# A new order of all steps for a fused attention and gMLP kernel, with 60 dense products issued as two halves of 64 columns

## The chip, the cores and the metric

The kernel runs on one core of one Trainium2 chip. The metric is the time of one execution in device microseconds; lower is better. Times given are medians of several runs.

## The reference

Two layers follow each other. The first is causal attention in a sliding window of 64 positions, for 8 batches, 8 heads, 576 positions and 64 features a head:

```python
scores = scale * np.matmul(q, k.transpose(0, 1, 3, 2))
mask = (rel >= 0) & (rel < window)
scores = np.where(mask, scores, -1000000000.0)
attn = np.exp(scores - max) ; attn = attn / sum
x = matmul(attn, v)                       # (8, 576, 512) after the heads are joined
```

The second is a gMLP block with a spatial gating unit:

```python
h = np.maximum(x @ w_in, 0.0)             # 512 -> 1024
u, v = h[..., :512], h[..., 512:]
v_n = (v - mu) / np.sqrt(var + 1e-06)
v_s = np.einsum('ts,bsd->btd', w_spatial, v_n) + b_spatial[None, :, None]
out = (u * v_s) @ w_out                   # 512 -> 512
```

Inputs and output are float32; the kernel computes its products in float16 with float32 sums.

## The kernel before, in words

A batch has 576 positions, handled as four blocks of 128 and a remainder of 64. Its work is cut into named steps, and each name carries the batch and the part:

- **ldk, ldq, ldv, ldx** load k, q and v (the first batch's v in two large pieces, ldx0_0 and ldx0_1, and a tail, ldv0_4). **ck, cq, cv, cx** cast to float16, **tk, tq** transpose on DVE (L433), **sl, su, s4** copy v into a second layout that is shifted by 64 rows, `hs`. For batch 0 a product with a picking matrix, **Y**, brings v into place, and **F** evicts it.
- **S** is q times k in tiles of 32 rows by 64 columns (64 products), **E** the exponential on ACT (L568), **M** the mask on DVE (L573). **Z** sums over the window with a matrix of ones (two products, one for each half of 64 columns), **N** and **n** on ACT turn the sum into its inverse by logarithm and exponential (L612, L614), **P** multiplies by v (16 products of 64 columns), and **X** on DVE scales the result (L605). Names that end in `_r` are the same steps for the remainder of 64 positions.
- **V** and **U** are the two halves of x times w_in, **Vr** and **Ur** their eviction with ReLU on ACT (L726, L828). **Vb** and **Va** are mean and variance on DVE (L728, L730), **L1** and **L2** the inverse deviation on ACT, **A** the normalisation on DVE (L799), which gives `vn`. **G** is the spatial product with `vn` as weights, **Ge** multiplies by u on DVE (L859), which gives `g`. **O** is the product with w_out, **Oe** its eviction (L703), **st** the store. V, U and O have four products of 128x128 weights by 512 columns, G has five. For batch 0, V is issued in two halves, V0a and V0b, of two products each.
- V of the remainder (V1_4, V2_4 and so on) has only 64 columns of weights. It shares its steps with the previous batch's remainder of O: the two stand side by side, one in partitions 0 to 63 of the bank, the other in 64 to 127.
- **W** transposes the spatial weights on PE (L384) out of their float16 copy (**cwsp**), **We** evicts them. **cwin** and **cwo** cast w_in and w_out. **D** is a product of zeros that does nothing but keep PE at work at the start (26 of them).

Nothing is left to a scheduler. `ORDER` is a long string of words, `step:engine:buffers`, and the kernel emits the steps just in that order, so that each engine's queue is the order of its words. `DQ` is SP's queue of loads and stores; `DG` is the same queue, with the transfer held until the product that stands last before it in the order has ended. The number behind the engine says which bank of the eight, or which buffer, the step takes. Every product goes through one helper, `mm` (L295), so that all of them carry this line in the profile; which step a row belongs to is read from its operands and its place.

Of the kernel before, what the change touches and what calls it, by code (L numbers as in the profile page):

```python
# [18 lines left out]
D0:PE:0 D1:PE:1 ldk0_0a:DQ:0 ldx0_0:DQ:0 D2:PE:2 ldk0_0b:DQ D3:PE:3 D4:PE:4 ldq0_0a:DQ:1 ldq0_0b:DQ  # L19
ldk0_1a:DQ:2 cq0_0a:POOL:0 D5:PE:5 pick:DVE:0 D6:PE:6 ck0_0a:ACT:1 D7:PE:7 D8:PE:0 tk0_0a:DVE:0  # L20
ldq0_1a:DQ:3 D9:PE:0 D10:PE:0 D11:PE:0 ck0_0b:ACT cx0_0:DVE:2 D12:PE:0 D13:PE:0 ldq0_1b:DQ D14:PE:0
ldk0_1b:DQ Y0_0:PE:0:1:2:3 cq0_0b:POOL F0_00:ACT:0 ldx0_1:DQ D15:PE:4 ck0_1a:POOL:3 tk0_0b:DVE
F0_01:ACT ldwsp0:DQ:4 D16:PE:4 D17:PE:4 ldwsp2:DQ:5 tq0_0a:DVE:1 F0_02:DVE D18:PE:4 tq0_0b:DVE
ldwsp1:DQ:6 ldwin10:DQ:7 ldv0_4:DQ D19:PE:4 F0_03:ACT D20:PE:4 cq0_1a:DVE:1 tk0_1a:DVE:2 D21:PE:4
cq0_1b:POOL tq0_1a:DVE:3 D22:PE:4 cwsp0:POOL ck0_1b:DVE ldwin11:DQ:0 tq0_1b:DVE D23:PE:4 D24:PE:4
D25:PE:4 S0_0:PE:4:5:6:7 E0_02:ACT:0 tk0_1b:DVE E0_03:ACT sl0_0x:ACT:0 E0_00:ACT:1 S0_1:PE:0:1:3:2
E0_01:ACT su0_0x:DVE M0_00:DVE cwin110:POOL ldq1_0:DG:1 cx0_1:ACT:2 E0_10:ACT:2 Y0_1:PE:6:7:4:5
ldk1_0:DG:3 M0_01:DVE Z0_01:PE:0 E0_12:ACT:3 F0_12:DVE E0_11:ACT F0_10:DVE cwin111:POOL
S0_r:PE:3:4:1:6 cwsp4:DVE E0_13:ACT E0_r0:ACT:0 M0_11:DVE ldwin01:DQ:2 Z0_00:PE:2 E0_r1:ACT
M0_10:DVE cwsp1:DVE E0_r2:ACT cwsp3:DVE F0_11:ACT cq1_0:POOL:0 cwsp2:DVE P0_00:PE:3 E0_r3:ACT  # L30
Z0_10:PE:4 N0_01:ACT:0 N0_10:ACT:1 Z0_11:PE:1 F0_13:ACT ldwin00:DQ:5 N0_00:ACT:2 M0_r:DVE P0_01:PE:7
W4:PE:6 W3:PE:0 sl0_1x:DVE cwin011:POOL n0_01:ACT su0_1x:DVE n0_00:ACT N0_11:ACT:3 P0_11:PE:4
n0_10:ACT cwin010:POOL cwin101:DVE Z0_r:PE:5 P0_10:PE:2 We3:DVE n0_11:ACT s40_:DVE X0_00:DVE:1
W1:PE:1 cwin100:ACT W0:PE:0 ldk1_1:DG:4 X0_01:DVE P0_r:PE:3 W2:PE:7 N0_r:ACT:4 cwin001:POOL
X0_10:DVE:2 ldq1_1:DQ:6 We4:DVE V0a_3:PE:5 We0:ACT X0_11:DVE ldb:DQ:7 V0a_2:PE:2 V0a_0:PE:0
ck1_0:ACT:1 We2:DVE tq1_0:DVE:4 V0b_2:PE ldwo0:DQ:0 tk1_0:DVE:5 We1:ACT V0b_3:PE n0_r:ACT V0a_1:PE:6
V0b_0:PE ldv1_0:DG:1 Vr0_2:ACT:0 X0_r:DVE:0 Vr0_0:ACT:1 ldv1_1:DG V0b_1:PE ldwo1:DQ:1
S1_0:PE:4:7:1:2 ldv1_2:DQ Vr0_3:ACT:2 cwin000:POOL Vr0_1:ACT:3 ldv1_3:DG Vb0_2:DVE:0 V0_4:PE:3
E1_00:ACT:1 Vr0_4:ACT:4 Vb0_0:DVE:1 Vb0_3:DVE:2 Va0_2:DVE E1_02:ACT:0 E1_03:ACT Vb0_1:DVE:3
U0_4:PE:0 Va0_3:DVE E1_01:ACT ldv1_4:DG ck1_1:POOL:3 Vb0_4:DVE:4 Va0_0:DVE Va0_1:DVE Va0_4:DVE  # L40
cb:POOL tk1_1:DVE:0 U0_3:PE:5 L10:ACT:0 ldk2_0:DG:3 L20:ACT U0_1:PE:6 Ur0_4:ACT:0 A0_2:DVE:0
cq1_1:ACT:2 U0_0:PE:4 cwo00:ACT U0_2:PE:3 ldq2_0:DQ:2 A0_0:DVE:1 A0_4:DVE Ur0_1:ACT:1 Ur0_0:ACT:2
Ur0_3:ACT:3 ldq2_1:DQ:5 A0_3:DVE:2 A0_1:DVE:3 tq1_1:DVE:1 cwo01:POOL Ur0_2:ACT:4 G0_0:PE:1
S1_1:PE:2:7:0:6 M1_01:DVE E1_10:ACT:3 E1_11:ACT Ge0_0:DVE:0 E1_12:ACT:2 G0_3:PE:4 S1_r:PE:5:3:1:2
E1_r0:ACT:1 E1_13:ACT M1_00:DVE cv1_0:DVE:1 M1_10:DVE Z1_01:PE:7 sl1_0:POOL:1 N1_01:ACT:5 Z1_00:PE:0
Z1_10:PE:5 E1_r1:ACT G0_1:PE:6 cwo11:POOL G0_4:PE:7 ldk2_1:DQ:4 Ge0_3:DVE:1 G0_2:PE:4 N1_10:ACT:2
M1_11:DVE Z1_11:PE:3 N1_00:ACT:0 su1_0:POOL n1_10:ACT ldq3_0:DG:7 E1_r2:ACT s41_:ACT ldk3_0:DG:6
# [6 lines left out]
Vr1_2:ACT:7 P1_r:PE:2 cq3_0:POOL:0 Vr1_1:ACT:0 Z1_r:PE:4 S2_1:PE:0:5:3:1 ldv2_4:DQ U1_3:PE:6
N1_r:ACT:3 n1_r:ACT M2_01:DVE E2_12:ACT:1 Vb1_1:DVE:5 X1_r:DVE:1 E2_10:ACT:0 ck3_0:POOL:3 V1_4:PE:7
E2_13:ACT Ur1_3:ACT:5 Vb1_0:DVE:0 Z2_00:PE:4 Z2_01:PE:3 Vb1_3:DVE:1 Vr1_4:ACT:1 Vb1_2:DVE:2
Va1_3:DVE U1_4:PE:2 N2_01:ACT:4 Vb1_4:DVE:1 U1_1:PE:0 Va1_0:DVE cv2_0:POOL:0 N2_00:ACT:2 Va1_1:DVE
ldq3_1:DG:0 E2_11:ACT U1_2:PE:1 Va1_2:DVE Va1_4:DVE L11:ACT:1 M2_11:DVE M2_10:DVE sl2_0:POOL:0
Ur1_4:ACT:2 L21:ACT ldk3_1:DQ:1 S2_r:PE:6:3:4:5 Ur1_1:ACT:3 A1_4:DVE ldv3_0:DG:1 A1_3:DVE:4
E2_r0:ACT:0 A1_1:DVE:5 Z2_11:PE:2 Oe0_4:ACT:0 A1_0:DVE:6 Z2_10:PE:0 N2_10:ACT:0 A1_2:DVE:7 s42_:ACT  # L60
E2_r1:ACT U1_0:PE:6 G1_1:PE:7 N2_11:ACT:1 ldv3_1:DQ cv2_1:POOL su2_0:POOL Ur1_0:ACT:1 E2_r2:ACT
G1_4:PE:0 tq3_0:DVE:4 Ur1_2:ACT:4 G1_0:PE:3 tk3_0:DVE:5 Ge1_4:DVE:5 ldv3_2:DG ldq4_1:DG:3
Ge1_1:DVE:6 su2_1:POOL sl2_1:ACT ldq4_0:DQ:2 ldv3_3:DQ S3_0:PE:2:6:4:1 E2_r3:ACT Ge1_0:DVE:7
P2_10:PE:0 M2_r:DVE n2_10:ACT P2_00:PE:7 n2_11:ACT n2_00:ACT st0_4:DQ P2_01:PE:5 E3_00:ACT:0
X2_10:DVE:1 st0_0:DQ n2_01:ACT cq3_1:POOL:1 X2_00:DVE:2 E3_01:ACT ldk4_0:DG:5 P2_11:PE:3 X2_11:DVE
ck3_1:ACT:2 ldv4_0:DG:0 G1_2:PE:0 X2_01:DVE Ge1_2:DVE:8 P2_r:PE:2 tq3_1:DVE:0 Z2_r:PE:7 cv3_0:POOL:1
ldv3_4:DQ N2_r:ACT:5 n2_r:ACT E3_02:ACT:3 G1_3:PE:3 tk3_1:DVE:1 V2_1:PE:6 Vr2_1:ACT:4 Vb2_1:DVE:0
V2_2:PE:5 sl3_0:POOL:1 V2_3:PE:0 Vr2_2:ACT:2 Ge1_3:DVE:9 Vr2_3:ACT:3 S3_1:PE:7:4:6:5 X2_r:DVE:0
U2_1:PE:3 E3_03:ACT E3_10:ACT:2 Vb2_2:DVE:1 S3_r:PE:0:2:1:7 M3_00:DVE E3_12:ACT:1 su3_0:POOL
E3_r0:ACT:1 M3_01:DVE E3_13:ACT Vb2_3:DVE:2 V2_4:PE:6 Z3_00:PE:0 M3_11:DVE E3_r1:ACT Z3_01:PE:5  # L70
Ur2_1:ACT:0 V2_0:PE:2 cv3_1:ACT Va2_3:DVE cq4_1:POOL:0 sl3_1:POOL Vr2_0:ACT:1 tq4_1:DVE:2 Va2_1:DVE
# [892 lines left out]
```

## Time and profile before

| | before |
|---|---|
| median of 3 runs | 199.34 us (199.3 to 199.66) |
| the profiled execution, span from first to last instruction | 197.1 us |
| PE busy | 186.1 us |
| DVE busy | 162.7 us |
| ACT busy | 161.9 us |
| POOL busy | 83.7 us |
| DMA | 42.67 MB, mean 217 GB/s |

The profiled execution is one run of its own; the span covers its instructions alone, 2.2 us less than the median of the timed runs. In a row of the timeline the first number is the start in us from the beginning of the span, the second the length; then come engine, line, operation, output and inputs, the size of the weight tile (rows*columns) for a product, and how many were merged into the row. In brackets stands the idle time before it and who ended it. Ends of products are modelled: a product of 512 columns is listed with 0.38 us, though the next one starts sooner. In the view by stretch, each engine has its busy time and in brackets its number of instructions; the last three numbers are the granted PE clock, the share of the DMA engines and GB/s.

### The profile page before, as it was taken

What the parts mean: (1) busy time and instruction counts of PE and PEld (TensorE: products, weight loads), DVE (VectorE), ACT (ScalarE), POOL (GpSimd) and SP (SyncE); (2) the same over time, 40 slices, a digit from 0 to 9 for tenths busy, and PEclk for the clock granted to TensorE, in tenths of its full rate; (3) what the DMA queues carried; (4) which work ended last, traced back from release to release, by engine and by line L of the source; (5) the groups of instructions that cost most, each with busy time, mean ns of one, the idle gap of its engine ahead of it and who ended that gap; (6) DMA issues with size and microseconds to landing.
All of it is one profiled execution on the core that took longest, in us unless ns stands there. A gap on an engine that the chain in (4) does not pass through costs nothing.

```text
span 197.1 us, 7044 instructions
## 1 busy us (share of the span) xinstructions
PE 186.1 (94%) x2935; PEld 98.1 (50%) x2935; DVE 162.7 (83%) x321; ACT 161.9 (82%) x342; POOL 83.7 (42%) x148
## 2 busy tenths in 40 slices
...
PEclk9995799999999999999999999999999999999999
...
GB/s 196 386 319 310 389 395 239 277 399 294 125 141 259 232 367 300 152 249 226 266 309 325 303 228 156 118 307 199 191 7 97 172 3 0 30 40 161 135 169 191
DMA packets 46977, 42.67 MB, mean 217 GB/s; under 512 B 34529, under 2 KB 35681, under 8 KB 46946
## 3 DMA queue, kind: packets, MB, share of 16 engines
...
q8 instruction: 23, 0.38, 0.8%
...
## 4 chain that ended last, share of the span: by engine, by line
PE 66%; ACT 19%; DVE 10%; issue 2%; POOL 1%
PE bank L295 66%; ACT e L568 6%; ACT vs L726 3%; ACT ru L828 3%; DVE e L573 2%; DVE x L605 2%; DVE g L859 1%; DVE hs L312 1%; ACT lz L612 1%; DVE vn L799 1%; ACT ob L703 1%; POOL hq L307 1%; DVE st L728 1%; DVE hv L312 1%; DVE qT L433 1%
## 5 line engine op out<-in xcount | busy, mean ns | idle before, releaser
L295 PE MATMUL bank<-wspT,vn 128*128 128x512 f16 (+3 forms) x320 | 43.1, 286 | 0.9 <-DVE vn L799 0.7
L295 PE MATMUL bank<-wout,g 128*128 128x512 f16 (+2 forms) x164 | 39.1, 375 | 0.3 <-DVE x L605 0.2
L295 PE MATMUL bank<-win,x 128*128 128x512 f16 (+1 forms) x160 | 38.6, 380 | 0.2 <-ACT e L568 0.2
L568 ACT ACTIVATE e<-bank 128x512 f16<-128x512 f32 x64 | 35.3, 603 | 3.3 <-PE bank L295 3.2
L295 PE MATMUL bank<-x,win 128*128 128x64 f16 (+1 forms) x256 | 35.0, 286 | 0.0
L859 DVE TENSOR_TENSOR g<-bank,ru 128x512 f16<-128x512 f32 (+1 forms) x40 | 24.1, 623 | 11.7 <-PE bank L295 7.0
L728 DVE BATCH_NORM_STATS2 st<-vs 128x6 f32<-128x512 f16 (+1 forms) x40 | 26.4, 679 | 8.9 <-ACT vs L726 8.7
L310 POOL COPY hs<-hv 64x512 f16<-64x512 f16 x38 | 25.4, 694 | 13.6 <-ACT hv L303 8.1
L295 PEld LDWEIGHTS <-vn 128*128 128x128 f16 (+1 forms) x320 | 20.1, 97 | 20.2 <-DVE vn L799 2.0
L703 ACT COPY ob<-bank 128x512 f32<-128x512 f32 (+1 forms) x39 | 22.9, 593 | 8.2 <-PE bank L295 7.9
L726 ACT ACTIVATE vs<-bank 128x512 f16<-128x512 f32 (+1 forms) x40 | 23.5, 607 | 4.4 <-PE bank L295 4.3
L828 ACT ACTIVATE ru<-bank 128x512 f32<-128x512 f32 (+1 forms) x40 | 21.2, 561 | 3.5 <-PE bank L295 3.4
L573 DVE TENSOR_TENSOR e<-e,mask 128x1024 f16<-128x1024 f16 x32 | 22.4, 720 | 1.7 <-ACT e L568 1.5
L295 PEld LDWEIGHTS <-win 128*128 128x128 f16 x256 | 15.8, 98 | 15.4 <-issue 1.5
L295 PEld LDWEIGHTS <-x 128*128 128x128 f16 (+1 forms) x160 | 14.9, 100 | 16.5 <-issue 0.8
L295 PEld LDWEIGHTS <-g 128*128 128x128 f16 (+1 forms) x164 | 15.0, 100 | 14.5 <-issue 0.4
L605 DVE TENSOR_TENSOR x<-bank,lz 128x512 f16<-128x512 f32 x32 | 20.5, 673 | 1.0 <-ACT lz L614 0.9
L433 DVE STREAM_TRANSPOSE kT<-hk 128x576 f32<-128x576 f32 (+1 forms) x18 | 20.2, 1121 | 1.0 <-ACT hk L303 1.0
L433 DVE STREAM_TRANSPOSE qT<-hq 128x576 f32<-128x576 f32 (+1 forms) x18 | 20.1, 1118 | 0.8 <-POOL hq L307 0.5
L307 POOL CAST hq<-nq 128x384 f16<-128x384 f32 x30 | 14.1, 505 | 14.9 <-DMA nq<-in_q_dram 8.8
L614 ACT ACTIVATE lz<-lz 128x512 f32<-128x512 f32 x32 | 19.9, 649 | 0.0
L307 POOL CAST hk<-nk 128x384 f16<-128x384 f32 x30 | 15.9, 567 | 9.3 <-DMA nk<-in_k_dram 9.2
...
## 6 DMA issues: line engine op xcount, KB each, us to landing
...
```

Source lines behind the costliest of these rows:

```text
L295: last[0] = nc.tensor.matmul(*a, **kw)
L307: nc.gpsimd.tensor_copy(o[:, n:n + w], i[:, n:n + w])
L310: nc.gpsimd.tensor_copy(o[:, c, :, :], i[:, c, :, :])
L433: lambda e, cs=cs, j0=j0, j1=j1: nc.vector.transpose(qt.t[:, :].rearrange("p (i j) -> p j i", j=18)[:, j0:j1, :], h.t[:, cs].bitcast(f32). ...
L568: lambda e, u=u, w=w: nc.scalar.activation(e2[u].t[:, w, :], sc[2 * u + w].t[:, :], AF.Exp, bias=0.0, scale=0.125),
L573: mins.append(add(f"M{b}_{g}{u}", ("DVE", 0.65), key, lambda e, u=u: nc.vector.tensor_tensor(e2[u].t[:, :, :], e2[u].t[:, :, :], mask[:, : ...
L605: lambda e, u=u, ob=ob, lz=lz: nc.vector.tensor_tensor(x.t[:, u, :], ob.t[:, :], lz.t[:, :], ALU.mult),
L703: lambda e: (nc.vector.tensor_copy if last else nc.scalar.copy)(view(), m.t[rows, 0:n]),
L726: rl = add(f"Vr{b}_{j}", ("ACT", 0.49), key, lambda e: nc.scalar.activation(vs.t[0:jn, :], m.t[0:jn, :], AF.Relu), deps=[pv], acq=[vs], us ...
L728: s1 = add(f"Vb{b}_{j}", ("DVE", 0.6), key + 0.02, lambda e: nc.vector.bn_stats(st6.t[0:jn, 0:6], vs.t[0:jn, :]), deps=[rl], acq=[st6], us ...
L828: lambda e, m=m, ru=ru, n=n: nc.scalar.activation(ru.t[:, 0:n], m.t[:, 0:n], AF.Relu), deps=[pu], acq=[ru], uses=[m])))
L859: lambda e, m=m, g=g, ru=ru, n=n: nc.vector.tensor_tensor(g.t[:, 0:n], m.t[:, 0:n], ru.t[:, 0:n], ALU.mult),
```

## The change

The words of `ORDER` are the same steps, with one D more (27 for 26), in another order throughout, and with other engines and buffers for some. At the start, the loads of batch 0 are issued in another order; the spatial weights stand ahead of w_in, as before, and batch 1's q now stands between the two pieces of w_in's V half. Many small steps, mostly of batch 0, are on other engines:

| from, to | steps |
|---|---|
| ACT to DVE, 15 | ck0_0a, F0_03, F0_11, F0_13, sl0_0x, We1, and nine Oe of batches 0, 2, 3, 4 and 5 |
| ACT to POOL, 17 | ck0_0b, cx0_1, cwin100, cwo00, cq1_1, cq2_0, ck3_1, ck4_1, cq6_1, cq7_0, cv3_1, cv5_1, sl2_1, su6_1, s41_, s42_, s44_ |
| DVE to ACT, 6 | cx0_0, F0_02, cq0_1a, ck0_1b, We4, su1_1 |
| DVE to POOL, 9 | cwsp3, cwsp4, sl0_1x, su0_1x, cwin101, s40_, cv1_0, cv1_1, sl1_1 |
| POOL to ACT, 6 | cwsp0, cwin011, cb, cv6_0, sl6_0, su7_0 |
| POOL to DVE, 3 | cwo01, cwo11, su1_0 |

Sixty of the V, U, G and O steps (8 halves of batch 0's V, and 52 others) carry the engine `PH` in place of `PE`. For these a new helper issues each product as two, with the left and the right 64 columns of the same weights, and the same moving operand, into the two halves of the bank's partitions. In PE's queue there are 3174 products in place of 2935: 238 from the pairs and one D. The eviction of O, Oe, may now be on DVE as well.

```diff
-S2_0:PE:2:0:4:3 Oe0_1:ACT V1_3:PE:5 Ge0_4:DVE:4 E2_00:ACT:3 V1_0:PE:1 tq2_1:DVE:0 E2_02:ACT:2
+O0_0:PH:7 Oe0_0:ACT:0 ck2_0:POOL:3 n1_11:ACT P1_11:PE:6 O0_1:PH:5 cq2_0:POOL:1 Z1_r:PE:4 O0_2:PH:2
...
-NWARM = 26
+NWARM = 27
...
+    def wide(e, o, w, x, **kw):
+        if e == "PE":
+            mm(o[:, :], w, x, **kw)
+        else:
+            for f in (0, 64):
+                mm(o[f:f + 64, :], w[:, f:f + 64], x, **kw)
...
-        last = (b, j) == (B - 1, 4)
-        cpy = add(f"Oe{b}_{j}", ("DVE", 0.4) if last else ("ACT", 0.49), key,
-                  lambda e: (nc.vector.tensor_copy if last else nc.scalar.copy)(view(), m.t[rows, 0:n]),
+        cpy = add(f"Oe{b}_{j}", [("ACT", 0.49), ("DVE", 0.6)], key,
+                  lambda e: cp(e, view(), m.t[rows, 0:n]),
...
                     for r in range(4):
-                        mm(m.t[:, :], xr(b, r)[:, 128 * j:128 * j + 128],
-                                         w_in_sb[r][:, 512:1024], start=(r == 0), stop=(r == 3))
+                        wide(e, m.t, xr(b, r)[:, 128 * j:128 * j + 128],
+                             w_in_sb[r][:, 512:1024], start=(r == 0), stop=(r == 3))
```

The same replacement of `mm` by `wide` is made in V0a and V0b, U (0 to 3), G (0 to 3) and O (0 to 3).

More of the change, by code (lines that the diff above doesn't have):

```diff
@@ L18 @@
 ORDER = """
[L19 to L47, printed above, removed]
@@ L54 @@
[L54 to L71, printed above, removed]
@@ new lines @@
+D11:PE:3 Y0_0:PE:4:5:6:7 D12:PE:0 ldx0_1:DQ D13:PE:1 F0_00:ACT:0 ck0_0b:POOL tq0_0a:DVE:2 tk0_0b:DVE
+D14:PE:2 ldb:DG:4 cq0_0b:POOL F0_01:ACT cq0_1a:ACT:1 F0_03:DVE ldwsp1:DG:5 tq0_0b:DVE ldwsp2:DG:6
+D15:PE:3 F0_02:ACT D16:PE:0 ldwsp0:DG:7 ck0_1b:ACT tq0_1a:DVE:3 S0_0:PE:4:1:5:2 D17:PE:3 E0_00:ACT:0
+ldv0_4:DQ sl0_0x:DVE:0 D18:PE:0 D19:PE:7 D20:PE:6 D21:PE:3 cq0_1b:POOL E0_01:ACT tq0_1b:DVE
+cx0_1:POOL:0 cwsp3:POOL tk0_1b:DVE su0_0x:DVE D22:PE:0 D23:PE:7 cwsp4:POOL E0_02:ACT:1 E0_03:ACT
+ldwin10:DG:1 S0_1:PE:6:4:3:0 E0_12:ACT:2 E0_10:ACT:3 E0_11:ACT Y0_1:PE:1:7:5:2 M0_00:DVE M0_01:DVE
```

216 lines of the change are left out of this document (128 added, 88 removed).

## Prediction

> **What bounds it now.** I read the page first, then the timeline of PE, then busy time by stretch.
>
> ```profile
> PE 186.1 (94%) x2935; PEld 98.1 (50%) x2935; DVE 162.7 (83%) x321; ACT 161.9 (82%) x342; POOL 83.7 (42%) x148
> PEclk9995799999999999999999999999999999999999
> PE 66%; ACT 19%; DVE 10%; issue 2%; POOL 1%
> ```
>
> PE is busy 94% of a span of 197.1 us and has two thirds of the last chain. A busy PE may still be a stalled one, since the ends of matmuls are modelled, so I go by start to start. The timeline of PE from 86 to 94 us, in batch 3 (columns: start, length, engine, line, operands, count):
>
> ```profile
> 88.13 1.24 PE L295 MATMUL bank<-wspT,vn 128*128 128x512 f16 x5
> 89.31 0.77 PE L295 MATMUL bank<-qT,kT 32*64 32x128 f16 x64
> 90.00 1.04 PE L295 MATMUL bank<-x,win 128*128 128x512 f16 x4
> 90.88 1.03 PE L295 MATMUL bank<-win,x 128*128 128x512 f16 x4
> 91.74 1.03 PE L295 MATMUL bank<-x,win 128*128 128x512 f16 x4
> ```
>
> Four matmuls of 512 columns take 91.74 - 90.88 = 0.86 us, so one takes 0.216. Five before S4_1 (89.31 - 88.13 = 1.18) would be 1.08; the rest, 0.10, is the price of going from tiles of 128x128 to tiles of 32x64. I call that a switch. S with the switch behind it is 0.69, so 0.585 alone.
>
> The timeline near 157 us shows the 64-column forms:
>
> ```profile
> 156.68 0.81 PE L295 MATMUL bank<-e,ones 128*64 128x512 f16 x6
> 157.33 0.29 PE L295 MATMUL bank<-er,hs 128*64 128x64 f16 x8
> ...
> 158.07 0.29 PE L295 MATMUL bank<-e,hv 128*64 128x64 f16 x6
> ...
> 158.33 0.29 PE L295 MATMUL bank<-e,hv 128*64 128x64 f16 x6
> ...
> 158.61 0.38 PE L295 MATMUL bank<-win,x 128*64 128x512 f16 x1
> 158.64 0.38 PE L295 MATMUL bank<-wout,g 128*64 128x512 f16 x1
> 158.83 0.38 PE L295 MATMUL bank<-win,x 128*64 128x512 f16 x1
> ...
> 159.48 0.41 PE L295 MATMUL bank<-e,ones 128*64 128x512 f16 x2
> 159.82 1.90 PE L295 MATMUL bank<-x,win 128*128 128x512 f16 x8
> ```
>
> A Z step (two products, one per half of the columns) takes (157.33 - 156.68) / 3 = 0.216, a P step 158.33 - 158.07 = 0.25. V6_4 is the row that matters most: two 64-column products start 0.03 us apart, the next pair 0.22 later, four pairs in 159.48 - 158.61 = 0.87. A pair side by side costs what one full product costs. Behind it Z7_11 has 0.34 in place of 0.22: a switch again, about 0.10 to 0.12. Between Z, P and V6_4 there is none.
>
> So the time is: PE's work, the switches, the waits, and the ends. From U0, PE has 92 steps of four 512-column products (0.8635, 79.4 us), 32 G (1.084, 34.7), 7 V_4 (6.0), 13 S (7.6), 28 Z (6.0), 28 P (7.1), and the small remainders (8 U_4, 8 G_4, 7 each of S_r, Z_r, P_r, and O7_4), 11.9 by their start-to-start times: 152.7 us. Counted along the order, there are 62 switches behind that point, 6.4 us at 0.103. U0 starts at 29.01 (row below) and the last product ends near 192.96, where 4.1 us of eviction, store and closing follow up to 197.1. The remainder, 163.95 - 152.7 - 6.4 = 4.85 us, is what PE waits in all of it: PE is nearly dense, and only three things can move the time by a microsecond: when U0 starts, the switches, the waits.
>
> **The pairs and the switches.** In PE's order before, batch 3's Z (e, ones) is followed by V2_0 with x as weights:
>
> ```order
> L295 LDWEIGHTS ones
> L295 MATMUL bank_67<-e_3_00_1722,ones 64x512
> L295 MATMUL bank_72<-e_3_01_1791,ones 64x512
> L295 LDWEIGHTS x_0_1732
> L295 MATMUL bank_69<-win_109,x_0_1732 128x512
> L295 MATMUL bank_69<-win_110,x_0_1732 128x512
> ```
>
> From 64 to 128 columns there: a switch. Now the same Z stand between U2_0 (win) and O1_1 (g), both as pairs:
>
> ```order
> L294 LDWEIGHTS win_112
> L294 MATMUL bank_67<-x_1_1758,win_112 64x512
> L294 LDWEIGHTS ones
> L294 MATMUL bank_71<-e_3_01_1861,ones 64x512
> L294 MATMUL bank_72<-e_3_00_1914,ones 64x512
> L294 MATMUL bank_73<-e_3_11_2002,ones 64x512
> L294 LDWEIGHTS g_0_1642
> L294 MATMUL bank_74<-wout_113,g_0_1642 64x512
> ```
>
> Attention goes in and out there with no switch. The whole new order has 68 switches against 78, and 51 against 62 from U0 on; with all products left whole it would have 135. So the pairs buy freedom of order: 11 x 0.103 = 1.1 us off, and small steps of attention can stand where they are ready. The 60 steps in pairs cost nothing by V6_4 (0.87 against 0.86); bounds are -0.00 and +0.024 us a step, the latter if each starts as after a switch: 1.4 us. I take 0, since most pairs stand beside other 64-column steps.
>
> A rule of the skill speaks against the pairs: the Trainium skill, TensorEngine Tiling (Array Packing), Restrictions and Gotchas, says that column tiling excludes the fast weight load. In this trace it costs nothing where loads hide: V6_4's pairs keep 0.22. By the rule alone, as an estimate from TensorE: Matmul & The Clock Gate, LDWEIGHTS (columns / 1.2 ns), two halves need 107 ns, still under the 216.
>
> **The start.** U0 needs V0, and V0 needs x and the halves of w_in. The rows of PE, POOL and DVE:
>
> ```profile
> 18.85 1.50 PE L384 MATMUL bank<-id,wnat 128*64 128x128 f16 x10
> 21.50 1.28 PE L384 MATMUL bank<-id,wnat 128*128 128x128 f16 x10
> 23.42 3.63 PE L295 MATMUL bank<-win,x 128*128 128x512 f16 x16
> ```
> ```profile
> 21.88 1.17 POOL L312 CAST win<-wi 128x512 f16<-128x512 f32 x2 [6.71 <-DMA wi<-in_moe_w_in_dram]
> 23.37 1.41 POOL L307 CAST hq<-nq 128x384 f16<-128x384 f32 x3 [0.32 <-DVE wspT L312]
> 27.43 1.17 POOL L312 CAST win<-wi 128x512 f16<-128x512 f32 x2 [0.15 <-DMA wi<-in_moe_w_in_dram]
> ```
> ```profile
> 17.41 1.34 DVE L312 CAST wnat<-ws 128x576 f16<-128x576 f32 x3
> 23.26 0.67 DVE L605 TENSOR_TENSOR x<-bank,lz 128x512 f16<-128x512 f32 x1
> ```
>
> The last spatial weights are cast by 18.75 and the transposes begin at 18.85. The second piece of w_in's V half lands at 21.88, the last piece of its U half at 27.4, when V0 has been under way since 23.42. In SP's queue before:
>
> ```order
> L336 DMA wi_213<-in_moe_w_in_dram 128x2x512
> L530 DMA nv_131<-in_v_dram 64x8x64
> L336 DMA wi_230<-in_moe_w_in_dram 128x2x512
> L424 DMA nq_0_378<-in_q_dram 128x1152
> L424 DMA nk_0_401<-in_k_dram 128x1152
> L336 DMA wi_451<-in_moe_w_in_dram 128x2x512
> ```
>
> and now:
>
> ```order
> L536 DMA nv_127<-in_v_dram 64x8x64
> L342 DMA wi_311<-in_moe_w_in_dram 128x2x512
> L430 DMA nq_0_402<-in_q_dram 128x1152
> L342 DMA wi_455<-in_moe_w_in_dram 128x2x512
> L430 DMA nk_0_465<-in_k_dram 128x1152
> L342 DMA wi_527<-in_moe_w_in_dram 128x2x512
> ```
>
> Batch 1's q (576 KB) has moved ahead of the second piece: at 390 GB/s (row below) 1.5 us later, 23.4. On POOL the order is now two casts of w_in, one of v, q's cast, then the second piece's casts:
>
> ```order
> L318 CAST win_110<-wi_311 128x512
> L318 CAST win_109<-wi_311 128x512
> L318 CAST hs_290<-nv_127 64x512
> L313 CAST hq_0_601<-nq_0_402 128x384 x3
> L318 CAST win_111<-wi_455 128x512
> L318 CAST win_112<-wi_455 128x512
> ```
>
> With the first piece at 20.7 (one load ahead of 21.9), 1.2 + 0.6 + 1.4 + 1.2 (rows above; v's cast as half of two w_in casts) end at 25.1. From there PE has V0's second halves (1.73), P0_r 0.12, V0_4 0.87, S1_0 0.585 and two switches, 3.5: U0 at 28.6. The first V0 halves and the transposes fit before 25.1, since the spatial weights land no earlier than now. One cast of w_in waits on ACT behind Vr0_1, some 0.1. I take 28.7, 0.3 earlier than 29.01; the bounds are 28.2 (the order of casts as quick as the U half's landing allows) and 30.2 (below).
>
> The clock decides inside these bounds:
>
> ```profile
> 8.68:12.09 3.41, 1.76 (x69) 0.91 (x67) 3.41 (x8) 1.55 (x3) 1.14 (x2) 1.00 1.07 383
> 12.09:15.51 3.42, 1.97 (x84) 1.47 (x85) 2.55 (x6) 3.42 (x7) 0.67 (x1) 1.00 1.05 294
> 15.51:18.92 3.41, 2.99 (x70) 2.00 (x70) 3.20 (x8) 2.90 (x10) 0.00 (x0) 0.50 1.10 281
> 18.92:22.33 3.41, 3.41 (x59) 2.59 (x54) 3.32 (x9) 3.41 (x8) 0.45 (x1) 0.50 1.04 390
> 22.33:25.74 3.41, 3.41 (x29) 1.85 (x29) 2.90 (x6) 2.09 (x4) 2.13 (x5) 1.00 1.04 391
> ```
>
> After a stretch with 1.97 us of thin products the granted clock is 0.50 for two stretches. Seven warming products now stand between S0_0 and S0_1, but from 12.1 to 15.5 PE has the same thin work and then waits for the spatial weights till 18.6. I expect the half clock again, from 15.5 or 18.9. If it lasts to 25.7 and beyond, V0 runs at half speed: 8 x 0.43 us more, of which about 1.5 aren't covered by the casts: 30.2. The small steps moved to other engines (cx0_0 to ACT, cx0_1 and the copies of v to POOL) lie under these waits and cost nothing while the spatial weights are what ends last; without that cover, cx0_1 on POOL would be two casts of 0.6 in place of about one.
>
> **The waits.** The first G stalls today:
>
> ```profile
> 29.01 4.09 PE L295 MATMUL bank<-x,win 128*128 128x64 f16 x32
> 32.94 0.38 PE L295 MATMUL bank<-wspT,vn 128*128 128x512 f16 x1
> 33.80 1.04 PE L295 MATMUL bank<-wspT,vn 128*128 128x512 f16 x4 [0.48 <-DVE vn L799]
> 34.96 0.77 PE L295 MATMUL bank<-qT,kT 32*64 32x128 f16 x64
> ```
>
> From 32.94 to 34.96 are 2.02 us for 1.18 of work: 0.84 lost to vn. PE's work between V0 and G0 grows from 4.0 to 5.1 us in the new order, so I take 0.45 of it back. The other 4.0 us I leave, bounded by 2 and 7.5, as the new order puts every step elsewhere.
>
> **The sum**: 28.7 + 152.7 + 51 x 0.103 (5.25) + 4.4 + 4.1 = 195.15 against 197.1, 1.9 us less. The median shown, 199.34, is 2.2 above the profiled span; so 197.4 us.
>
> **Rivals.** *DVE becomes the bound* (slower). DVE is the fullest engine in the middle:
>
> ```profile
> 60.00:70.00 10.00, 9.83 (x253) 5.80 (x252) 10.00 (x17) 9.14 (x19) 5.80 (x11) 1.00 0.97 242
> 120.00:140.00 20.00, 19.74 (x359) 10.84 (x358) 18.38 (x33) 19.53 (x41) 9.42 (x19) 1.00 0.73 208
> ```
> ```profile
> L859 DVE TENSOR_TENSOR g<-bank,ru 128x512 f16<-128x512 f32 (+1 forms) x40 | 24.1, 623 | 11.7 <-PE bank L295 7.0 <-ACT vs L726 2.5 <-ACT ru L828 2.1
> ```
>
> Nine output evictions move from ACT to DVE, six before 145 us: at 0.62 (as Ge, the nearest row that reads 512 columns of a bank) 3.7 us, while w_out's casts come and v's go, about even. If DVE has no gap for them, x, vn and g all come that much later: 195.15 + 3.7 = 198.9, or 201.1 us. It decides once DVE's idle time, 1.6 of 20 us in the second row and none in the first, is used up. Against it: PE seldom waits for DVE today, and ACT, which feeds DVE, gives up 32 steps and takes 12. 0.17.
>
> *The waits just eat the gain*: they grow by about 2 us instead of shrinking, 199.3. 0.06.
>
> *The waits go*: with pairs the small steps stand where they are ready, and ACT has lost work; 2 us of the 4.4 vanish, 195.4. 0.13.
>
> *Pairs are dearer*: both halves now read the same moving tile, which no row shows. At 0.024 us on each of 238 pairs that is 5.7 us, 203.1. 0.04.
>
> **Chances.** My forecast has 0.60, of which 0.03 lies within 0.2% of before, about what a measurement of this kernel can tell from no change. Faster: 0.57 + 0.13 = 0.70; same: 0.03 + 0.06 = 0.09; slower: 0.17 + 0.04 = 0.21. The range goes from the vanishing waits, 195.4, nearly to the DVE case, 200.9.
>
> **What would show it.** Right: four pairs in 0.86 to 0.87 us; U0 starting at 28.2 to 29.2; Z and P beside pairs without the 0.10; G0 with a stall under 0.5. Wrong: pairs spaced by over 0.23; idle time before PE named x, e or vn on DVE that adds up to over 6 us from U0 on; a half clock beyond 25.7.

## The result, and the profile after

| | before | after |
|---|---|---|
| median of 4 runs each | 199.5 us (199.3 to 200.06) | 209.89 us (208.25 to 211.22) |
| ratio | | 1.05 (95%: 1.0445 to 1.0555) |
| span of the profiled execution | 197.1 us | 209.4 us |
| U0 starts | 29.01 us | 29.96 us |
| waits of PE from U0 on | 4.85 us | 17.7 us |

The kernel got slower by 5%, far outside the range and the other way than forecast. Executions that came out over 1.5% above the fastest of their kernel (seven in the runs below: six of 208.26 to 219.54 us and one of 365.58) are left out of the times and ratios, and where such an execution was the traced one (block edges moved in the new kernel, spatial weights' loads at once), its trace is used for places.

The waits are worked out as in the prediction: the last product ends at 205.6, U0 starts at 29.96; less 152.7 of work and 5.25 of switches, 17.7 us remain. That is 12.85 us more than before; the span grew by 12.3.

The page of the new kernel:

```profile
PE 187.0 (89%) x3174; PEld 101.9 (49%) x3174; DVE 172.1 (82%) x324; ACT 151.2 (72%) x322; POOL 103.7 (50%) x182
PEclk9999699999999998899999999999999999999999
q8 instruction: 24, 0.39, 0.9%
PE 55%; DVE 24%; issue 7%; ACT 6%; DMA 4%; SPq 1%; POOL 1%; POOLq 0%; DVEq 0%; ACTq 0%
```

PE has 89% of the span where it had 94. In the last chain DVE has 24% (it had 10) and "issue", time in which an engine waits for nothing that the profile shows, 7% (it had 2, of a shorter span). The waits from 29 to 95 us say whose issue it is (columns: waited in total, times, longest):

```profile
PEld L294 <- issue: 13.1, 18, 3.8
...
PE bank L294 <- issue: 5.8, 2, 3.7
...
PE bank L294 <- DVE er L652: 2.2, 1, 2.2
```

PE's weight loads show 13.1 us of it in 18 pieces. Many are the short gaps of a switch, but two are not, as the timeline of the weight loads in batch 3 shows:

```profile
70.18 0.53 PEld L294 LDWEIGHTS <-kT 32*64 32x64 f16 x49 [0.41 <-DVE x L611]
73.00 0.15 PEld L294 LDWEIGHTS <-kT 32*64 32x64 f16 x15 [2.29 <-issue]
...
77.73 0.15 PEld L294 LDWEIGHTS <-kT 32*64 32x64 f16 x13 [0.42 <-issue]
81.66 0.17 PEld L294 LDWEIGHTS <-kT 32*64 32x64 f16 x19 [3.78 <-issue]
```

Inside S3_0, behind its 49th product of 64, PE stops for 2.3 us, and inside S3_r, behind its 13th of 32, for 3.8 us. The profile shows no semaphore that the product behind either gap waits for: k and q are there, and the products ahead of it use the same tiles. Counted along PE's queue (a weight load and a matmul are two instructions), the gaps stand at numbers 2239 and 2495, 256 apart. Section 3 of the page has a queue for instructions, q8, with 24 packets of 16 KB; the 6348 instructions of PE's products are 24.8 times 256. I call an edge every place in PE's queue whose number leaves 191 when divided by 256 (one or two less in some of the runs below). In the records of q8 there is one packet to each edge; most start behind it, a few up to 2.2 us ahead of it. The times say that it is the block behind the *next* edge:

| kernel | edge passed | packet on the queue | next edge reached | PE goes on |
|---|---|---|---|---|
| before | 62.26 | 63.8 to 64.7 | 69.3 | at once |
| before | 69.33 | 72.9 to 73.9 | 78.4 | at once |
| after | 66.89 | 70.7 to 71.6 | 70.60 | 73.00 |
| after | 70.60 | 78.6 to 80.1 | 77.78 | 81.66 |

So PE has one block ahead of the one it is in; it stops where it reaches the end of that before the next has come. The runs below show this too: from U0 on, their traces and this one have 24 stops of over 1 us at such an edge, and each ends 1.2 to 1.8 us after the packet that belongs to the edge before has landed. In the new kernel the packets come 4 and 8 us after their edge, and the edges are only 3.7 and 7.2 us apart, since an S step runs through 128 instructions in 0.6 us. The DMA queues are full just then (the change also makes 24 loads of the kernel wait for a product that didn't before, and lets 20 go at once that did). By stretch, of the new kernel (PE busy first, the last three numbers are clock, DMA share and GB/s):

```profile
60.00:70.00 10.00, 9.33 (x149) 5.17 (x145) 9.89 (x20) 8.35 (x21) 5.54 (x11) 1.00 1.01 345
70.00:80.00 10.00, 5.83 (x180) 3.19 (x177) 8.78 (x14) 5.09 (x10) 8.19 (x15) 1.00 1.15 287
```

PE works 5.83 of 10 us in the second row. Behind the longer stop the granted clock falls to half for about 3 us:

```profile
81.90:85.10 3.20, 3.20 (x29) 1.44 (x20) 0.00 (x0) 1.35 (x3) 2.92 (x7) 0.55 1.07 300
```

The Trainium skill, Runtime: NRT & Kernel Launch, Instruction fetch mechanics, says that each engine's sequencer gets its instructions in blocks of 256 through a DMA queue of its own, and that crossing a block is "mostly hidden". The trace agrees on the 256; here the crossing isn't hidden, with 2.3 and 3.8 us.

The second loss is on DVE, in batch 1. The timelines of DVE and of POOL:

```profile
44.44 0.67 DVE L611 TENSOR_TENSOR x<-bank,lz 128x512 f16<-128x512 f32 x1
45.03 3.44 DVE L652 TENSOR_TENSOR er<-er,maskr 128x512 f16<-128x512 f16 x1
```
```profile
44.87 0.61 POOL L318 CAST hs<-nv 64x512 f16<-64x512 f32 x1
45.43 1.41 POOL L313 CAST hk<-nk 128x384 f16<-128x384 f32 x3
46.79 1.41 POOL L313 CAST hq<-nq 128x384 f16<-128x384 f32 x3
```

M1_r, a mask of 0.4 us, stands for 3.44 us, until POOL has done seven casts in a row (46.79 + 1.41 = 48.20; the mask ends at 48.47). Z1_r on PE waits 2.4 us for it, from start to start (the row above that names DVE er has 2.2, by modelled ends), and S2_0 0.9 more, as its transposes stand behind the mask on DVE. The Trainium skill, SBUF — State Buffer, Who interferes with whom, says that a DVE instruction with two SBUF inputs contends with a GpSimd instruction that reads SBUF. The trace agrees on who is held; the mask waits through seven instructions of POOL.

So the 17.7 us are 6.4 of stops at block edges (2.34, 3.83 and 0.24), 1.5 of half clock behind them (seven pairs, each 0.21 later than at full clock), 3.3 of the held mask, and 6.5 of other waits, where before had 4.85 in all. In this trace the three named causes are 11.2 of the 12.85 us that came on top.

### The profile page after: what moved, and what is told of

Same layout as the page of the kernel before. It is cut to its first block, busy times and chain, and to the rows that moved or that the text cites. A ratio compares the mean times of both kernels' runs of the same rounds, so it can differ in the third digit from the quotient of the medians.

```text
span 209.4 us, 7553 instructions
## 1 busy us (share of the span) xinstructions
PE 187.0 (89%) x3174; PEld 101.9 (49%) x3174; DVE 172.1 (82%) x324; ACT 151.2 (72%) x322; POOL 103.7 (50%) x182
## 4 chain that ended last, share of the span: by engine, by line
PE 55%; DVE 24%; issue 7%; ACT 6%; DMA 4%; SPq 1%; POOL 1%; POOLq 0%; DVEq 0%; ACTq 0%
PE bank L294 54%; DVE e L579 5%; DMA ws<-in_moe_w_spatial_dram 4%; DVE g L864 3%; DVE st L733 3%; DVE x L611 3%; DVE kT L439 2%; DVE vn L804 2%; DVE qT L439 2%; DVE er L652 2%; PE bank L390 1%; ACT vs L731 1%; ACT e L574 1%; ACT lz L620 1%; ACT lz L618 1%
## 5 line engine op out<-in xcount | busy, mean ns | idle before, releaser
L294 PE MATMUL bank<-wspT,vn 128*64 128x512 f16 (+5 forms) x390 | 44.1, 303 | 1.2 <-DVE vn L804 1.2
L294 PE MATMUL bank<-wout,g 128*64 128x512 f16 (+2 forms) x212 | 41.1, 389 | 0.1
L294 PE MATMUL bank<-win,x 128*64 128x512 f16 (+1 forms) x212 | 39.8, 384 | 0.0
L294 PE MATMUL bank<-x,win 128*128 128x64 f16 (+2 forms) x324 | 36.9, 308 | 0.0
L313 POOL CAST hq<-nq 128x384 f16<-128x384 f32 x42 | 22.6, 573 | 22.9 <-DVE qT L439 9.6
L294 PEld LDWEIGHTS <-vn 128*128 128x128 f16 (+3 forms) x390 | 21.2, 102 | 19.0 <-DVE vn L804 3.4
L294 PE MATMUL bank<-qT,kT 32*64 32x128 f16 (+2 forms) x1280 | 16.1, 220 | 10.2 <-issue 6.9
L294 PEld LDWEIGHTS <-win 128*128 128x128 f16 (+1 forms) x324 | 17.7, 104 | 13.8 <-issue 1.1
L294 PEld LDWEIGHTS <-g 128*64 128x64 f16 (+1 forms) x212 | 16.2, 108 | 13.0 <-issue 1.6
L294 PEld LDWEIGHTS <-x 128*64 128x64 f16 (+1 forms) x212 | 15.4, 106 | 14.4 <-issue 0.4
L294 PEld LDWEIGHTS <-kT 32*64 32x64 f16 x1280 | 12.8, 103 | 19.7 <-issue 11.6
L618 ACT ACTIVATE lz<-bank 128x512 f32<-128x512 f32 x32 | 18.8, 602 | 3.0 <-PE bank L294 3.0
```

The costliest lines, as they stand in the source:

```text
L294: last[0] = nc.tensor.matmul(*a, **kw)
L313: nc.gpsimd.tensor_copy(o[:, n:n + w], i[:, n:n + w])
L618: a = add(f"N{tag}", ("ACT", 0.06 + 0.00083 * n), key, lambda e: nc.scalar.activation(lz.t[:, 0:n], zb.t[:, 0:n], AF.Ln), deps=[z], acq=[l ...
```

## The experiments

Theory A: stops at block edges, and held masks. Rival B: DVE has too much work in the new order. Rival C: the pairs themselves cost the time. Each run's ratio is that to the kernel before on the same chip. The new kernel's own times spread over 3 us, so a difference of 1 us between two runs says little.

**Two casts from POOL to ACT.**

```diff
-ck2_1:POOL:2
+ck2_1:ACT:2
-cq2_1:POOL:0
+cq2_1:ACT:0
```

> The casts ck2_1 and cq2_1 of batch 2 go from POOL to ACT, nothing else. Theory A (in the new order PE loses its time at a few places: it stops for its own instructions inside S3_0 and S3_r, 2.3 and 3.8 us and about 1.5 us of half clock behind them, and M1_r on DVE stands still for 3 us while POOL works through a run of casts): M1_r takes 0.4 to 0.6 us in place of 3.44, Z1_r no longer waits 2.4 us, the stops in batch 3 stay, and the time falls by 2 to 4 us, to 206 to 208. Rival B (DVE has more work than it can do in time, so the new order is late everywhere): M1_r gets short but the wait comes back within the next steps, time within 1 us of 209.9. Rival C (the pairs cost the time): no change.

Measured: 207.39 us (206.33 to 208.22), ratio 1.037 (1.029 to 1.045), 2.5 us less than the new kernel. M1_r takes 0.70, Z1_r doesn't wait; the stops are there (2.3 and 2.5). This is as theory A has it, though the second trace of the new kernel, below, shows that M1_r is not held each time. New is a wait of 1.9 us at G4_3 (134.5 us): k of batch 7 lands late, and DVE's transpose of it stands ahead of the normalisation.

**Two loads later.**

```diff
-... ldk3_1 ldv3_3 ldk5_1 ldk4_1 ... ldk6_0 ldv4_0 ...
+... V2_4 ldk5_1 ...  ldk6_1 ldk6_0 ...
```

> Two loads that are needed late, ldk5_1 (issued at 62 us, cast at 92) and ldk6_0 (issued at 71 us, cast at 91), move behind V2_4 and behind ldk6_1 in the order; nothing else. Theory A, with the stops of PE's instructions coming from its instruction transfers standing behind data in the DMA queues: the stops inside S3_0 and S3_r (2.3 and 3.8 us) shrink to under 1 us each, the half clock behind them goes, time 209.9 less 4 to 8, 202 to 206. Rival B (DVE's work is the bound): PE waits at the same places for DVE instead, within 1 us of 209.9. Rival C (the pairs cost the time): no change.

Measured: 212.6 us (212.38 to 213.71), ratio 1.065 (1.057 to 1.072), slower. Both theories' forecasts fail. The stop in S3_r is gone (the packet behind the edge in S3_0 now starts 3.9 us after it, in place of 8.0), that in S3_0 stays at 2.0, and a new wait of 4.9 us stands at 91.6. The timeline of ACT names it:

```profile
87.70 1.57 ACT L309 COPY ob<-bank 128x512 f32<-128x512 f32 x3
94.97 1.15 ACT L309 CAST hk<-nk 128x1152 f16<-128x1152 f32 x1 [5.71 <-DMA nk<-in_k_dram]
```

ACT waits 5.7 us for the load that I moved, with the exponentials of S4 behind it. The edit was too blunt to test the queue; it shows that these loads have no slack.

**Both edits together.**

> The two casts of batch 2 on ACT and the two loads later, together. Theory A: both gains add, 7 to 11 us off, 199 to 203. Rival B: what is gained at one place is lost at the next, 207 or more. Rival C: no change.

Measured: 214.73 us (213.91 to 215.0), ratio 1.075 (1.066 to 1.083), where theory A forecast 199 to 203: the wait on ACT again, and stops of 2.8 and 0.6. Nothing more follows from it.

**Block edges moved.** The cleanest test of the stops: nothing of the work changes place, only its number in PE's queue.

```diff
 # at the start of W1, whose transposes wait for the spatial weights
+for _ in range(64):
+    nc.tensor.matmul(m.t[:, 0:1], id16[:, :], scratch[:, 0:1], start=True, stop=True)
```

> 64 extra products of one column (128 instructions) stand in PE's queue ahead of W1's transposes, where PE waits 2.4 us for the spatial weights; they write a place that W1 overwrites. All else as in the new order. Theory A: the stops come at every 256th instruction of PE's queue (number 191 of 256), so none comes inside S3_0 and none inside S3_r at the old products; the place that was number 2111 (G1_3) and the one that was 2367 (S3_1) are now at the edge of a block, and a stop, if the transfer is late there, is inside G1_3 or S3_1. Time anywhere between 202 and 211. Rival B or C, or a stop that belongs to the data of S3_0 and S3_r: both stops stay at their products, 2.3 and 3.8 us, time 209 to 212.

Measured: 204.73 us (204.18 to 204.97), ratio 1.024 (1.015 to 1.032): half of the loss is gone, by adding instructions. The weight loads in its trace:

```profile
69.10 0.65 PEld L294 LDWEIGHTS <-kT 32*64 32x64 f16 x64 [0.41 <-DVE x L615]
...
74.38 0.22 PEld L294 LDWEIGHTS <-kT 32*64 32x64 f16 x32 [0.42 <-issue]
...
80.52 1.65 PEld L294 LDWEIGHTS <-win 128*64 128x64 f16 x17 [1.18 <-issue]
...
94.51 0.43 PEld L294 LDWEIGHTS <-kT 32*64 32x64 f16 x40 [1.81 <-issue]
```

S3_0 runs through its 64 products and S3_r through its 32. The larger stops are now inside P0_10 (22.6, 1.5 us), P1_11 (45.4, 1.3), U2_2 (79.3, 1.1) and S4_1 (92.7, 1.8): all at edges, at products that had none in the new kernel. So the stops belong to the place in the queue, not to the data.

**Less data on the queues.**

```diff
+ds = slice(1024, 1152) if b >= 3 else cs
-n.t[:, cs], src...[:, cs]
+n.t[:, ds], src...[:, ds]        # the cast reads n.t[:, 1024:1152] nine times
```

So from batch 3 on it leaves out eight ninths of k and q.

> All steps and their order as in the new kernel; from batch 3 on each load of k and q brings only the last 128 of its 1152 columns and the cast reads these nine times, so that the wrong k and q are used there and the DMA queues carry some 17 MB less. Theory A (PE stops because its instruction blocks stand behind data in the DMA queues): the blocks come within 2 us of their request, the stops inside S3_0 and S3_r are under 0.5 us each, no half clock after them, M1_r on DVE in batch 1 still takes about 3.4 us; 201 to 204 us. A rival cause of the same stops (PE's queue simply can't be filled faster than some pace, whatever the DMA does): both stay, over 2 us each. Rival B (DVE's work is the bound): within 1.5 us of 209.9. Rival C (the pairs cost the time): no change.

Measured: 204.56 us (203.89 to 206.19), ratio 1.028 (1.022 to 1.033). The DMA queues moved 32.2 MB for 42.7. The edges and their products are the same as in the new kernel, and now:

```profile
68.18 0.65 PEld L294 LDWEIGHTS <-kT 32*64 32x64 f16 x64 [0.41 <-DVE x L619]
...
73.44 0.22 PEld L294 LDWEIGHTS <-kT 32*64 32x64 f16 x32 [0.42 <-issue]
```

There is no stop in either (one of 1.25 us is in S2_0, at 48.5). The packets come 1.0 and 1.8 us after the edges at 64.89 and 68.60, for 3.8 and 8.0. With the shift, this shows both halves of the cause: where the edge stands, and how late its block comes when the queues carry data. The gain is about 5 us, no more, and just misses the forecast of 201 to 204. M1_r, forecast to stay at 3.4 us, takes 0.44, but another mask is held now: in batch 3, 3.0 us for 0.65, and PE waits 1.4 for it.

```profile
74.65 3.04 DVE L587 TENSOR_TENSOR e<-e,mask 128x1024 f16<-128x1024 f16 x1
```

**No pairs.** Every `PH` as `PE`.

> The new order with every PH as PE: no product is issued as a pair, 476 PE instructions less. The order then has 135 switches of tile form in place of 68, 6.9 us at 0.103. Theory A: the pairs themselves cost nothing, so whole products win nothing and the switches come on top; ahead of S3_0 are 118 instructions less, so the block edges fall elsewhere and the 7.7 us of stops in batch 3 may go or stay: 208 to 217. Rival C (the pairs cost the time): faster than 205 in spite of the switches. Rival B (DVE's work is the bound): PE's switches lie in its waits, 208 to 211, with the stops replaced by waits for DVE.

Measured: 209.86 us (207.95 to 210.49), ratio 1.050 (1.044 to 1.056), the same time as with the pairs. It has 67 switches more (6.9 us) and no stop in batch 3 (118 instructions less ahead of it); its one large wait is at the start, where a mask of batch 0 is held while POOL works without a gap from 18.4 to 25.4:

```profile
18.56 6.34 DVE L579 TENSOR_TENSOR e<-e,mask 128x1024 f16<-128x1024 f16 x2
```

U0 starts at 34.5 there, 4.5 us later than in the new kernel, so the equal time is chance. From U0 to the last product it takes 169.2 us for 175.6. By the prediction's sum, with 113 switches (11.6 us) in this stretch, PE waits 4.9 us in it, as much as before, with the same DVE work and in the same order. So that work alone doesn't make the new order late, though a later U0 also gives the loads more time. Whether the pairs cost time can't be told from this run, since 476 instructions went with them and the edges moved. The next run asks that.

**Pairs alone, in the order of before.**

> The order, the engines and the buffers of before; only the 60 steps that are pairs in the new kernel are issued as pairs here too. That order then has 99 switches in place of 78, 2.2 us at 0.103, and 476 PE instructions more. Theory A: pairs cost nothing by themselves: 199.5 + 2.2 = 201.7, and 0 to 4 us more where a block of instructions now ends in a bad place (a stop at number 191 of 256); 201 to 206. Rival C (the pairs cost the time): the whole loss of 10 us is here, 207 to 212. Rival B (DVE's work in the new order): 201 to 202, no stops.

Measured: 204.86 us (203.18 to 205.61), ratio 1.025 (1.019 to 1.031): 5.3 us, of which 2.2 are switches; stops of 1.3 us at 64.9 and 1.0 inside S3_r at 72.4, 256 instructions apart, are 2.3 more. That leaves under 1 us for 238 pairs. Theory A's range holds it, and rival C falls.

**Nine evictions back on ACT.** Oe0_1, Oe2_0 and seven more from `DVE` to `ACT`.

> The nine evictions of O that the change moved from ACT to DVE (Oe0_1, Oe2_0, Oe2_1, Oe3_1, Oe3_2, Oe4_1, Oe5_1, Oe5_2, Oe5_4) go back to ACT, nothing else: 5.6 us less for DVE, as much more for ACT. Theory A (stops of PE's instructions and one blocked mask): within 1.5 us of 209.9, stops and the 3.4 us of M1_r as before. Rival B (DVE's work is the bound, of which these nine are the new part): 203 to 207. Rival C (the pairs cost the time): no change.

Measured: 207.27 and 207.57 us, ratio 1.039 (1.035 to 1.044), about 2 us less than the new kernel, between the two forecasts. The stops are there (1.8 and 2.1), M1_r is not held (0.59). From U0 to the last product its trace takes 4.5 us less than the new kernel's; the mask that happened not to be held (3.3) and the shorter stops are more than that, so nothing is left that only DVE's work would explain.

**The new kernel again.**

> The new kernel once more, unchanged, for a second trace. Theory A: PE stops at the same two products, the 191st of a block of 256 inside S3_0 and inside S3_r, by 1.5 to 4 us each; whether M1_r on DVE is blocked by POOL's casts for 3 us, as in the first trace, or takes 0.4 to 0.7 us, as in the run with the nine evictions on ACT, depends on when the casts' loads arrive and may differ: with the block a span near 209, without it near 206.5. Rival B (DVE's work is the bound) names no places: PE's waits lie elsewhere than in the first trace.

Measured, one execution: 211.51 us. The stops are at the same two products, 1.8 and 3.0 us:

```profile
71.77 0.15 PEld L294 LDWEIGHTS <-kT 32*64 32x64 f16 x15 [1.79 <-issue]
...
79.61 0.23 PEld L294 LDWEIGHTS <-kT 32*64 32x64 f16 x19 [2.95 <-issue]
```

M1_r takes 0.65, but the span is still 209.8, against the forecast of 206.5 for that case: now two masks of batch 0 are held, 3.87 for 1.3, and U0 starts at 32.2 instead of 30.0.

```profile
18.41 3.87 DVE L579 TENSOR_TENSOR e<-e,mask 128x1024 f16<-128x1024 f16 x2
```

The stops are fixed to their place, the held masks are not.

**Block edges moved in the kernel before.** The same 64 products, ahead of S0_1.

> The kernel before with 64 extra products of one column ahead of S0_1, where PE waits 2.2 us for batch 0's k and q; nothing else is changed. Theory A: the edges of PE's instruction blocks come 64 products earlier in the program. With edges spaced by 2.7 to 3 us near U0 and near P2 of batch 2, and a transfer that takes 4 to 5 us when the queues are full, the kernel before gets stops it did not have: about 2 us at U0_4 (30 us), 1 us in S2_1 (54 us) and 3 us in batch 2's P steps (66 us), time 201.5 to 205. Rival (where the blocks end does not matter, the new order itself is late): 199 to 200.

Measured: 208.0 us (206.41 to 208.53), ratio 1.040 (1.034 to 1.047): some 8 us slower with every step in its old order, over the forecast's 205. A stop is inside P2_11, as forecast:

```profile
65.61 0.12 PEld L295 LDWEIGHTS <-hs 128*64 128x64 f16 x2
68.45 0.11 PEld L295 LDWEIGHTS <-hv 128*64 128x64 f16 x2 [2.71 <-issue]
```

From U0 to the last product it takes 4.5 us more than before (168.4 against 163.95): this stop, and the half clock that follows it for 3.4 us. Another 3.1 us are lost ahead of U0 (32.1 for 29.0). There the trace has a stop that the forecast did not name: inside S0_1, behind its 54th product, PE waits 3.5 us at the edge with number 447, until 17.09, 1.45 us after a packet has landed. The added products make S0_1 0.6 us later as well, and half clock lasts from 14.7 to 24.9; how the 3.1 us divide among these isn't shown. The stops forecast at U0_4 and S2_1 didn't come.

**The spatial weights' loads at once.** `DG` to `DQ` for the three.

> The new kernel with the three loads of the spatial weights issued without waiting for products (they were held until the product ahead of them in the order had ended). Theory A for the start (U0 is 0.95 us late because the spatial weights land later and their transposes start at 19.55 us in place of 18.85): the transposes start 0.5 to 1 us earlier, U0 at 29.0 to 29.5 in place of 29.96, and the time falls by that, 208.5 to 209.5, if the stops in batch 3 stay as they are. Rival for the start (the half clock makes U0 late): U0 stays at 29.9.

Measured: 206.46 and 209.38 us, ratio 1.042 (1.032 to 1.052). In the trace the transposes start at 19.22, 0.3 earlier, not 0.5 to 1, and U0 at 31.2, later, with half clock through V0. The forecast gain of about 1 us is less than the two traces of the new kernel differ in U0, so nothing can be read from this run.

**All mended.**

> The new order with all that the runs so far name: 72 extra products ahead of W1 (block edges out of S3_0, S3_1 and S3_r), ck2_1 and cq2_1 on ACT, su0_1x and sl0_1x back on DVE, the spatial weights' loads at once. Theory A: U0 at 29.5, no mask blocked for over 1 us, stops under 2 us in all; what stays are waits for late loads near G4 (1.8 us) and smaller ones: 200.5 to 203.5, so still not faster than before. Rival B (DVE's work is the bound): 205 or more.

Measured: 206.36 us (205.71 to 207.71), ratio 1.035 (1.029 to 1.041). Theory A's forecast fails by about 3 us, and the time is on rival B's side. The trace speaks for the causes of theory A all the same. No mask of batches 0 and 1 is held and the stops in batch 3 are gone, and from U0 to the end of the last product it takes 168.7 us against 175.6. But U0 starts at 31.5, 2.5 later than before, behind half clock for 10.2 us (6.8 before); four smaller stops stand at other edges (0.5 to 1.0 us, 3.2 in all); Z5 waits 1.5 for a mask that takes 1.53 in place of 0.65, and G4 0.9 for vn. PE's rows have 2.6 us of waits for DVE from U0 on, for 1.3 before.

**The moves between engines undone,** 56 steps, without and with 72 products for the edges.

> The new order and its pairs, but each small step that the change moved to another engine is back on the engine it had before (56 steps). Theory A: the stops inside S3_0 and S3_r stay (4 to 6 us with the half clock), masks on DVE are no longer held for over 1 us by long POOL runs; ACT gets 4 steps of 32 back and DVE loses some, so some new waits for ACT: 205 to 209. Rival B (DVE's work is the bound): 203 to 206 and no stops. If the moves between engines were what made the order work, it gets slower: over 211.

> The same with 72 extra products of one column ahead of W1, which take the block edges out of S3_0, S3_1 and S3_r. Theory A: both causes gone or small, 201 to 204. If the blocked masks come from the order and not from the engines: 204 to 207, with a mask on DVE of over 1.5 us in the trace.

Measured: 213.57 us (213.13 to 214.71), ratio 1.070 (1.065 to 1.076), and 217.79 us (216.6 to 219.06), ratio 1.091 (1.085 to 1.097). Both are slower than the new kernel and far above theory A's forecasts (205 to 209 and 201 to 204); as the first expectation says for a time over 211, the moves between engines earn some 4 us in this order. A mask is held here too, in batch 3 (3.0 us at 84.5), with every small step on its old engine: the order is enough for that, against the first forecast. With the shift the stops in batch 3 shrink, but U0 starts at 33.4, and PE waits 3.2 us at G4_3 for vn.

**A POOL run alone,** of eleven copies, and then of one copy and fourteen casts, in the kernel before.

> The kernel before; behind M7_01 (about 153 us) POOL gets eleven copies of 128x512 float16 in a row, some 6 us, which nothing waits for; POOL is idle there otherwise. Theory A (a mask, which reads two operands from SBUF, waits for the whole run of POOL): the next mask on DVE (M7_10 or M7_00) takes 2 to 6 us in place of 0.65 and ends with the run; steps that read a bank keep their 0.4 to 0.7. Rival (DVE and POOL take turns, instruction by instruction): no mask over 1.3 us.

> The kernel before; behind M7_01 POOL gets one copy and fourteen casts from float32 to float16 of 128x288 in a row, some 6 us, which nothing waits for. If it is casts from float32 that hold a mask (theory A as it stands): M7_10 or M7_00 takes over 1.5 us in place of 0.65, through three or more casts. Rival (a mask gets its turn at the next gap between two POOL instructions, whatever they are): no mask over 1.2 us, and what was seen in the new kernel is luck at the gaps.

Measured, one execution each; DVE and POOL with the copies:

```profile
153.58 1.98 DVE L574 TENSOR_TENSOR e<-e,mask 128x1024 f16<-128x1024 f16 x2
```
```profile
152.72 8.06 POOL L580 COPY scratch<-scratch 128x512 f16<-128x512 f16 x10
```

and with the casts:

```profile
154.39 1.50 DVE L574 TENSOR_TENSOR e<-e,mask 128x1024 f16<-128x1024 f16 x2
```
```profile
153.41 8.13 POOL L580 CAST wnat<-wnat 128x288 f16<-128x288 f32 x14
```

Two masks inside the run take 1.98 and 1.50, for 1.27 before: held for one instruction at most. POOL is what suffers (0.81 a copy, for 0.62 of the single copy ahead of it). Theory A's forecast falls twice; the rival, turns at the gaps, holds here. So these two runs don't reproduce the held masks, and what makes a mask miss up to eight gaps in the new order stays open. (Both executions are 7 to 8 us longer, since a step of batch 7 stands behind the run on POOL and PE waits 5.9 us for it.)

**Three pairs in the order of before.** U1_3, G1_2 and U4_2 from `PE` to `PH`.

> The order of before with three steps as pairs, U1_3, G1_2 and U4_2, each of which stands between steps of 64 columns: 74 switches in place of 78, 26 PE instructions more. Theory A: 4 x 0.103 = 0.4 us off, 199.1, if no block edge falls badly. Rival C (pairs cost): 199.5 or more.

Measured, 12 runs: 201.22 us (200.01 to 202.19), ratio 1.0075 (1.0044 to 1.0105): a small loss, but clear of 1. It is slower by 1.7 us with four switches less and 26 instructions more, which is rival C's forecast by its number. But a stop that wasn't there stands inside O3_3:

```profile
132.40 0.20 PEld L295 LDWEIGHTS <-g 128*128 128x128 f16 x2
133.84 1.17 PEld L295 LDWEIGHTS <-g 128*128 128x128 f16 x6 [1.24 <-issue]
```

From U0 to the last product the trace takes 1.1 us more than before. The stop is all of that; the rest of the longer span is a later U0 (30.45 for 29.01), ahead of which the edit changes nothing.

**The two edits that gained alone.**

> The new order with 64 extra products ahead of W1 (alone: 204.85) and ck2_1 and cq2_1 on ACT (alone: 207.39 against 209.9), nothing else. Theory A (stops at block edges and a held mask are separate causes): the gains add, 209.9 - 5.0 - 2.5 = 202.4, between 201.5 and 203.5. If they overlap, since the shift also changes when the casts run: 204 to 205. Rival B (DVE's work is the bound): 204 or more, with PE waiting for DVE at G4 and Z5.

Measured: 208.38 us (206.63 to 208.98), ratio 1.045 (1.039 to 1.051). The gains don't add; the casts' 2.5 us are lost and most of the shift's 5 too. Its trace has stops of 2.0 in U2_2 and 1.2 in S4_1, at the shifted edges, and M5_r held for 2.6. Each edit also moves when loads are issued, and with that, I take it, which block comes late and which mask meets casts; no run separates this.

No kernel of these beats the one before, so there is no better version to show.

## Why the prediction was wrong, point by point

- **"A pair side by side costs what one full product costs": right.** Timeline of PE, after:

```profile
103.73 1.03 PE L294 MATMUL bank<-x,win 128*64 128x512 f16 x8
104.59 0.28 PE L294 MATMUL bank<-er,ones 128*64 128x128 f16 x4
104.70 1.03 PE L294 MATMUL bank<-win,x 128*64 128x512 f16 x8
105.57 0.23 PE L294 MATMUL bank<-e,hv 128*64 128x64 f16 x4
```

  Four pairs in 0.86 and 0.87, on both kinds of weights, and no 0.10 between them and their 64-column neighbours. "The 60 steps in pairs cost nothing" was still wrong as a whole: they are 476 instructions more in a queue that is fetched in blocks. Pairs in the order of before cost about 3 us beyond their switches, 2.3 of them in stops, and three pairs alone made it 1.7 us slower, 1.24 of it a stop, where a gain of 0.4 was due.
- **The switches: right in number.** In the traces the products change their tile form 62 times from U0 on before and 51 times after, as counted. No run tests their price by itself.
- **U0 at 28.7: came at 29.96,** inside its bounds of 28.2 and 30.2, but outside the 28.2 to 29.2 that would have shown the prediction right. "The spatial weights land no earlier than now" passed over that they could land later. Their loads were issued 2.2 us later than before. DVE and PE, after:

```profile
18.82 0.66 DVE L318 CAST wnat<-ws 128x576 f16<-128x576 f32 x1 [1.72 <-DMA ws<-in_moe_w_spatial_dram]
```
```profile
19.55 1.48 PE L390 MATMUL bank<-id,wnat 128*128 128x128 f16 x15 [1.09 <-ACT wnat L309]
```

  The transposes start at 19.55 for 18.85, V0 at 24.15 for 23.42. That the later landing made U0 late is argued, not shown: the run with these loads issued at once did not bring U0 earlier. The half clock came as expected (0.77 and 0.73 in the two stretches from 18.92). The second trace has U0 at 32.2: what was one number is a spread of 2 us.
- **G0's stall under 0.5: wrong,** 1.03. The five normalisations ahead of it took 2.81 us where they took 1.97 before, beside POOL's casts of q and v.
- **"The other 4.0 us I leave": the step that failed.** The sum's 4.4 us of waits became 17.7: 6.4 of stops at the edges of PE's instruction blocks, 1.5 of half clock behind them, 3.3 of a held mask, 6.5 of others. The upper bound of 7.5 had no mechanism behind it, only the size of what was there. I had read PE's waits as waits for other engines. The trace of before shows no stop over 0.5 us at a block edge, and so I took PE's own queue as free: the sum has no term for it and gives no reason; but its packets were there to see (23 in q8 on the page of before), as was a DMA share of 0.97 from 60 to 70 us, and the count of instructions in PE's queue, which the change raises from 5870 to 6348. That the block behind the edge at 69.33 comes 3.6 us after it in before, and the next edge only after 9 us, was the margin to look at. That before has no such stop is in part luck of its order, as the 64 added products show.
- **The rivals.** DVE as the bound (201.1) was on the right side for another reason: its nine evictions account for 2 us at most, and the sign set for it did not come, since PE's rows name x, e or vn on DVE for 2.8 us from U0 on, not for over 6. What DVE adds to PE's waits is in large part masks that stand still (2.2 us more are named er). *Pairs are dearer* was priced per product, 0.024; most of what pairs cost in two runs stands at block edges. No rival had a transfer of instructions in it.
